# A spectral filter and an expert layer on one core: the first block's down matmuls by quarters, four input loads at other steps, one turn ahead of a piece

## The chip, the core and the metric

The kernel runs on one core of a Trainium2 chip. The metric is the device time of one execution in microseconds (us); the reference is the median of three executions of the kernel before, 767.72 us. The engines are TensorE (PE in the profile; PEld is its weight load), VectorE (DVE), ScalarE (ACT), GpSimd (POOL) and SyncE (SP). Here POOL computes next to nothing: it issues one queue of DMAs (the input loads, the swaps of the filter product), and SP issues the other (tables, transposing round trips through DRAM, output stores).

## The reference

Two layers, one behind the other. The first filters every channel of every batch in the frequency domain; the second is a feed-forward layer with a learned slope below zero.

```python
X = np.fft.rfft(x, axis=1)                    # x: 8 batches, 3008 rows, 256 channels
F = (filt_r + 1j * filt_i)[None, :, :]
y = np.fft.irfft(X * F, n=x.shape[1], axis=1)

h = y.reshape(24064, 256) @ w_in              # 256 -> 2048
g = np.maximum(h, 0.0) + alpha * np.minimum(h, 0.0)
return (g @ w_out).astype(np.float32)         # 2048 -> 256
```

## The kernel before

The transform of 3008 points is split into 94 times 32, and each part is done as matmuls with constant tables. For one batch the pieces are, in order: **a** (94-point part, eight pieces of two matmuls, evicted by ScalarE into `asb`, written to DRAM by `save_a` and read back transposed by `turn_a` into `at`), **b** (32-point part, six pieces; VectorE multiplies the result with the filter twice, into `ww` and `uu`, and POOL issues four DMAs that bring the halves of `ww` to the other partitions: for batch 1 they add straight into `uu`, the argument `direct` of `piece_b`), **c** (inverse 32-point part, six pieces), a second round trip through DRAM (`turn_c`), and **d** (inverse 94-point part, `pair_d`), which leaves the filtered rows transposed in `yT`.

Batch 0 has a class of its own, `First`, that turns its data on TensorE in place of DRAM: `piece_t` and `half_t` turn, `half_d` and `pair_d` are its last stage, `first_d` the beginning of that stage.

The feed-forward layer runs over 48 blocks of 512 or 384 rows of `yT` (`Block`). A block's `up` has 16 steps; each multiplies by one slice of 128 columns of `w_in`, and after every second one ScalarE copies two banks to `gtb` (line 586); after every fourth VectorE has made one group of four slices of g (lines 589 and 591). There are thus four groups, and group i holds the slices k = 4i to 4i+3 that the down matmuls need. The very first block is different: `up4` goes through its 512 rows in two halves, so that its four groups become ready one after another at the very end of its steps (lines 608, 613 and 614).

A block's down matmuls, 16 slices k for each of four lanes `si` of 128 rows, 64 in all, are cut into 16 **units** of four matmuls, which stand in the list `todo` and are done between the ups of the next block. Before, a pair of lanes is done at a time: lane 0 with k = 0 to 7, lane 1 with k = 0 to 7, lane 0 with k = 8 to 15, lane 1 with k = 8 to 15, then lanes 2 and 3 in the same way. A pair has one PSUM bank (`op`, from the pool `psO` with two), which ScalarE copies to `osb` when the pair is done, and SP then stores it.

Everything is in an order written out by hand: the program's global **step** runs on from block to block, 16 to a block, and `plan[step]` lists the pieces of the transforms that are put in front of that step's up. Engines take their instructions in that order and each waits for its own inputs. From step 16 to 149 one unit of the block before is done at every step. What a step puts into the plan stays in the order of the `put` calls: within one step batch 1's entries come ahead of batch 2's. `load_x` (line 123 for batches 1 to 3) issues two DMAs on the POOL queue, each of 192 KB (fp16), for half of the rows of a chunk; a batch has four chunks, chunk c being read by the pieces a number 2c and 2c+1. The pool `p_x` has four buffers, so a chunk's buffer comes free when the chunk of the same number of the batch before has been through its two pieces.

The steps that matter here, as `plan_fft` is called before:

| what | steps |
|---|---|
| batch 1, pieces a; save and turn | 16, 18, ... 30; 30 and 31 |
| batch 1, pieces b | 40, 46, 52, 58, 63, 68 |
| batch 1, pieces c | 52, 58, 64, 70, 76, 80 |
| batch 2, loads of chunks 0 to 3 | 32, 40, 50, 56 |
| batch 2, pieces a | 48, 54, 60, 66, 72, 74, 82, 84 |
| batch 3, loads of chunks 0 to 3 | 57, 69, 113, 123 |
| batch 3, pieces a | 106, 112, 118, 124, ... |

Of the kernel before, what the change touches and what calls it, by code (L numbers as in the profile page):

```python
# [11 lines left out]
FP32 = mybir.dt.float32  # L12
# [5 lines left out]
D = 256  # L18
# [3 lines left out]
AF = mybir.ActivationFunctionType  # L22
# [33 lines left out]
def kernel(  # L56
# [10 lines left out]
    nc = tc.nc  # L67
# [13 lines left out]
    psO = ctx.enter_context(tc.tile_pool(name="psO", bufs=2, space=bass.MemoryType.PSUM))  # L81
# [34 lines left out]
    def load_x(b, c, held=False):  # L116
        xs = p_x.tile([128, 8 * D], FP16, name="xs")
        if held:
            for r in (slice(0, 32), slice(64, 96)):
                nc.vector.memset(xs[r, 0:2], 0.0)  # L120
        if b:
            for r in (slice(0, 48), slice(48, N1)):
                nc.gpsimd.dma_start(out=xs[r], in_=xrow(b, c)[r])  # L123
        else:
            w = 8 * D // (1 + (c == 3))
            for o in range(0, 8 * D, w):
                nc.gpsimd.dma_start(out=xs[0:N1, o : o + w], in_=xrow(b, c)[:, o : o + w])
        return xs

    def load_halves(b, c):  # L130
        lo, hi = (p_x.tile([128, 8 * D], FP16, name="xs") for _ in range(2))
        nc.gpsimd.dma_start(out=lo[0:48], in_=xrow(b, c)[0:48])
        if b + 1 < NB:
            nc.gpsimd.dma_start(out=hi[0:48], in_=bass.AP(
                tensor=x.tensor, offset=x.offset + (b * NFFT + 47 * N2 + 8 * c) * D, ap=[[N2 * D, 48], [1, 8 * D]]))
        else:
            nc.gpsimd.dma_start(out=hi[0:32], in_=xrow(b, c)[47:79])
            nc.gpsimd.dma_start(out=hi[32:47], in_=xrow(b, c)[79:94])
        return lo, hi
# [26 lines left out]
    class Fft:  # L166
        def __init__(self, b):
            self.b = b
            self.base = (b % 2) * NFFT
            self.wi = wi3_s if b else wif_s  # L170
            self.uw = {}
# [290 lines left out]
    f0 = First()  # L462
# [89 lines left out]
    def store(p, t0, osb, lane):  # L552
        t = t0
        while t < t0 + 128:
            b, r = 2 * p + t // NFFT, t % NFFT
            g, o = r // NX, r % NX
            n = min(t0 + 128 - t, NX - o)
            row = b * NFFT + (o // 4) * N2 + 4 * g
            nc.sync.dma_start(
                out=bass.AP(tensor=out.tensor, offset=out.offset + row * D,  # L560
                            ap=[[N2 * D, n // 4], [D, 4], [1, D]]),
                in_=osb[t - t0 : t - t0 + n, lane])
            t += n
# [3 lines left out]
    class Block:  # L567
        def __init__(self, p, t0, tn):
            self.p, self.t0, self.tn = p, t0, tn
            self.gts, self.gs = [], []  # L570

        def up(self, j):
            tn = self.tn
# [40 lines left out]
                nc.vector.tensor_add(g, g, m)  # L614
                self.gts += [g[:, h] for h in range(4)]

        def start_down(self, last):
            n = self.tn // 128
            ends = [2, 3, 4] if last else list(range(2, n, 2)) + [n]
            half = 12 if last else 8  # L620
            self.todo = []
            for s0, s1 in zip([0] + ends, ends):
                for ks in (range(half), range(half, 16)):
                    self.todo += [(s0, s1, si, k) for si in range(s0, s1) for k in ks]

        def down(self, q):
            n = self.tn // 128
            for s0, s1, si, k in self.todo[n * q : n * (q + 1)]:
                if si == s0 and k == 0:
                    self.op = psO.tile([128, 2, D], FP32, name="op")  # L630
                nc.tensor.matmul(self.op[:, si - s0], self.gts[k][:, 128 * si : 128 * si + 128],  # L631
                                 wout_s[:, k], start=(si == s0 and k == 0), stop=(si == s1 - 1 and k == 15))
                if k == 15 and si == s1 - 1:
                    m = s1 - s0
                    osb = p_osb.tile([128, 2, D], FP32, name="osb")
                    nc.scalar.activation(osb[:, 0:m], self.op[:, 0:m], AF.Copy)  # L636
                    for lane in range(m):
                        store(self.p, self.t0 + 128 * (s0 + lane), osb, lane)

# [2 lines left out]
    def put(step, fn, *args):  # L642
        plan.setdefault(step, []).append((fn, args))

    def put_h(step, fn, *args):
        put(step, fn, *args)
        psum[step] = psum.get(step, 0) + 1

    def plan_fft(b, a_at, ta, x_at, b_at, add, c_at, d_at):
        f = Fft(b)  # L650
        split = b > 3
        for q in range(6):
            put_h(c_at[q], f.piece_c, q)
            if q % 2 == 1:
                put(c_at[q] + 1, f.turn_c, q // 2)
        for q in range(6):
            put(b_at[q], f.piece_b, q, not add)
            if add:
                put(b_at[q] + add, f.piece_s, q)
        for i in range(8):  # L660
            put_h(a_at[i], f.piece_q if split else f.piece_a, i)
        for c in range(4):
            put(a_at[2 * c + 1] + split, f.save_q if split else f.save_a, c)
            if b in (2, 3):
                put(x_at[c], lambda b=b, c=c: xc.update({(b, c): load_x(b, c, b == 3 and c > 1)}))
            if split:
                x0, x1, x2 = x_at[c]
                put(x0, lambda b=b, c=c: xc.update({(b, c): load_halves(b, c)}))
                put(x1, f.less, c)
                put(x2, f.plus, c)  # L670
        w = NK // len(ta)
        for q, t in enumerate(ta):
            put(t, f.turn_a, nc.sync, w * q, w * q + w)
        for i in range(8):
            put(d_at[i], f.pair_d, i, on_act)
# [5 lines left out]
        nc.vector.tensor_scalar(alm_s, al_s, 1.0, -1.0, OP.mult, OP.add)  # L681

    put(1, f0.half_d, 1, on_act, "o")
    put(1, f0.half_d, 3, on_dve, "o")
    put(1, f0.piece_t, 2, on_dve)
    for i in (6, 7):
        put(3, lambda i=i: on_dve(*f0.half_t(i, "o")))
    put(7, f0.pair_d, 2, on_dve)
# [12 lines left out]
    def d_steps(p):  # L701
        return [p + t for t in (92, 94, 104, 108, 116, 120, 140, 152)]

    plan_fft(1, range(16, 32, 2), [31] * 4, None, (40, 46, 52, 58, 63, 68), 0, (52, 58, 64, 70, 76, 80),
             (93, 95, 98, 101, 114, 121, 142, 154))
    plan_fft(2, (48, 54, 60, 66, 72, 74, 82, 84), [90] * 4, (32, 40, 50, 56),
             (106, 116, 126, 136, 148, 158), 7, (116, 126, 136, 148, 158, 172), d_steps(96))
    for b in range(3, NB):
        p = 96 * (b - 1)
        if b == 3:  # L710
            a_at = (106, 112, 118, 124, 130, 132, 140, 144)
            x_at = (57, 69, 113, 123)
            ta = (155, 166)
        else:
            a_at = [p - 96 + t for t in (-34, -22, 2, 2, 14, 26, 38, 50)]
            x_at = [[p - 96 + t for t in r] for r in
                    ((-66 if b == 4 else -68, -52, -40), (-32, -18, -10), (-20, -4, 8), (4, 20, 32))]
            ta = (p - 39, p - 28)
        plan_fft(b, a_at, ta, x_at, range(p + 2, p + 74, 12), 8, range(p + 14, p + 86, 12), d_steps(p))
# [8 lines left out]
    last = 0  # L728
    blk = Block(0, 0, 512)
    for step in range(16):  # L730
# [4 lines left out]
                     8: [lambda i=i: f0.half_d(i, on_dve, "o") for i in (6, 7)]}.get(step, []))  # L735
        for fn, args in plan.pop(step, ()):
            fn(*args)
    blk.start_down(False)
    units.extend((blk, q) for q in range(16))
    step = 16  # L740

    for p, t0, tn in blocks[1:]:
        blk = Block(p, t0, tn)
        for j in range(16):
            n = psum.get(step, 0)
# [9 lines left out]
            if n:  # L755
                last = step
# [39 lines left out]
```

## Time and profile before

| what | value |
|---|---|
| three executions | 767.60, 767.72, 771.18 us; median 767.72 us |
| the profiled execution | 768.86 us |
| its span, first to last instruction | 767.1 us |
| TensorE busy | 756.9 us |
| VectorE busy | 633.9 us |
| ScalarE busy | 583.3 us |
| costliest line: down matmuls, 3008 | 431.1 us, 273 ns each |
| next: up matmuls, 1504 | 418.1 us, 375 ns each |
| DMA: SP's queue and POOL's queue | 69.50 MB and 29.49 MB |

The span is 1.8 us shorter than the execution's time; what lies around it is the same small start and end. All times below that look like a place (at 80.01) are microseconds from the span's start. Matmuls overlap in the array, so the mean time of one is longer than the distance from one start to the next: a group of four matmuls with 512 columns has 0.86 us from its start to the start of what follows, one of four with 256 columns 0.43 us, when nothing holds them up. A wait of TensorE is therefore read from the distance of two starts, against the same group elsewhere.

### The profile page before, as it was taken

The numbers are of one execution on the slowest core, as the hardware profiler recorded it, in microseconds if no ns is written. First come the engines' busy times: TensorE is split into PE (matmuls) and PEld (weight loads), VectorE is DVE, ScalarE is ACT, GpSimd is POOL, SyncE is SP. The second block draws the span as 40 slices with busy tenths as digits, with TensorE's granted clock in tenths as the row PEclk, the third lists the DMA queues.
The fourth block names the chain that finished last, engine by engine and source line by source line (L and its number), as shares of the span: only waits on it lengthen the run. The fifth ranks groups of instructions, "written<-read, shape, count | busy, mean of one in ns | idle before, by whom it ended". The sixth has DMA issues, their size and how long they took to land.

```text
span 767.1 us, 16602 instructions
## 1 busy us (share of the span) xinstructions
PE 756.9 (99%) x6553; PEld 507.3 (66%) x6553; DVE 633.9 (83%) x1163; ACT 583.3 (76%) x672; POOL 147.0 (19%) x277
## 2 busy tenths in 40 slices
PE   8999999999999999999999999999999999999998
PEld 4666657666666666666666666766666666766666
DVE  4898975889889998899978998999877888666663
ACT  4788788888778777887778787787777777776664
POOL 6610840221211220121202122022101212000000
PEclk9999999999999999999999999999999999999999
DMA  9996996665752559533774438544463223510111
GB/s 162 157 225 173 175 204 181 166 171 139 178 153 69 139 142 197 143 97 97 188 205 96 125 104 179 166 97 118 131 162 87 71 68 97 152 36 28 42 42 56
DMA packets 97486, 100.04 MB, mean 130 GB/s; under 512 B 12086, under 2 KB 83398, under 8 KB 97216
## 3 DMA queue, kind: packets, MB, share of 16 engines
q1 hardware_dynamic: 82384, 69.50, 31.1%
q0 software_dynamic: 15024, 29.49, 21.4%
q8 instruction: 51, 0.84, 0.4%
q14 instruction: 27, 0.22, 0.1%
HBM read 55.02 MB, written 46.66 MB: 133 GB/s over the span
## 4 chain that ended last, share of the span: by engine, by line
PE 91%; DMA 4%; POOL 2%; DVE 1%; ACT 1%; issue 1%; SPq 0%; POOLq 0%; DVEq 0%; ACTq 0%
PE op L631 41%; PE hps L577 40%; PE psF L291 3%; PE hps L269 2%; PE psF L238 1%; PE hps L184 1%; DMA xs<-in_x_dram 1%; DMA uu<-ww 1%; PE hps L210 1%; DMA a_dram<-asb 1%; PE hps L600 1%; POOL filt_s L147 1%; DMA filt_s<-in_filt_r_dram 1%; POOL uu L250 1%; ACT asb L313 0%
## 5 line engine op out<-in xcount | busy, mean ns | idle before, releaser
L586 ACT ACTIVATE gtb<-hps 128x1024 f16<-128x1024 f32 (+1 forms) x376 | 377.9, 1007 | 132.6 <-PE hps L577 129.7
L631 PE MATMUL op<-wout_s,gtb 128*128 128x256 f16 x3008 | 431.1, 273 | 0.6 <-DVE gtb L614 0.6
L577 PE MATMUL hps<-yT,win_s 128*128 128x512 f16 (+1 forms) x1504 | 418.1, 375 | 0.3 <-ACT asb L313 0.2
L631 PEld LDWEIGHTS <-gtb 128*128 128x128 f16 x3008 | 290.8, 98 | 164.8 <-issue 10.7
L589 DVE TENSOR_SCALAR m<-gtb,alm_s 128x512 f16<-128x512 f16 (+1 forms) x752 | 227.3, 346 | 97.6 <-ACT gtb L586 96.1
L591 DVE TENSOR_TENSOR gtb<-gtb,m 128x2048 f16<-128x2048 f16 (+1 forms) x188 | 226.1, 1203 | 10.4
L577 PEld LDWEIGHTS <-win_s 128*128 128x128 f16 x1504 | 142.5, 98 | 54.9 <-issue 5.3
L252 POOL DMA_DIRECT2D sw<-ww x144 | 71.8, 506 | 414.2 <-DVE ww L245 399.4
L636 ACT ACTIVATE osb<-op 128x512 f32<-128x512 f32 (+1 forms) x97 | 56.6, 583 | 12.3 <-PE op L631 10.9
L313 ACT ACTIVATE asb<-hps 128x1024 f16<-128x1024 f32 (+1 forms) x56 | 56.7, 1020 | 6.4 <-PE hps L184 4.8
L245 DVE TENSOR_TENSOR ww<-psF,filts_s 128x1024 f16<-128x1024 f32 x42 | 51.2, 1219 | 1.0 <-DMA uu<-ww 0.7
L313 ACT ACTIVATE v<-hps 128x1024 f16<-128x1024 f32 (+1 forms) x43 | 43.5, 1012 | 11.2 <-PE hps L269 11.1
L246 DVE TENSOR_TENSOR uu<-psF,filt_s 128x1024 f16<-128x1024 f32 x42 | 51.1, 1216 | 0.0
L313 ACT ACTIVATE yT<-psF 128x752 f16<-128x752 f32 (+1 forms) x59 | 46.5, 788 | 1.7 <-PE psF L291 1.5
L291 PEld LDWEIGHTS <-zt 96*128 96x128 f16 x504 | 28.0, 98 | 5.8 <-issue 0.4
L291 PE MATMUL psF<-wi_s,zt 96*128 96x94 f16 x448 | 27.9, 205 | 0.0
L257 DVE TENSOR_TENSOR uu<-uu,sw 128x1024 f16<-128x1024 f16 x36 | 24.6, 683 | 1.3 <-DMA sw<-ww 1.3
L250 POOL DMA_DIRECT2D uu<-ww x24 | 19.6, 1174 | 28.1 <-DVE uu L246 21.4
L123 POOL DMA_DIRECT2D xs<-in_x_dram x24 | 17.6, 1009 | 12.9 <-DMA win_s<-in_moe_w_in_dram 4.5
L194 DVE TENSOR_TENSOR xs<-xs 47x2048 f16<-47x2048 f16 x16 | 19.5, 1219 | 0.4
L198 DVE TENSOR_TENSOR xs<-xs 47x2048 f16<-47x2048 f16 x16 | 19.4, 1210 | 0.0
L269 PE MATMUL hps<-uu,twi_s 64*64 64x256 f16 x336 | 17.6, 281 | 0.2 <-DMA uu<-ww 0.2
(99 smaller groups left out, 264.8 us busy)
## 6 DMA issues: line engine op xcount, KB each, us to landing
out_dram<-osb SPq DMA_DIRECT2D x128, 128.0 KB
v_dram<-v SPq DMA_DIRECT2D x84, 128.0 KB
zt<-v_dram SPq DMA_DIRECT2D x28, 384.0 KB
sw<-ww POOLq DMA_DIRECT2D x144, 64.0 KB, 2.7
xs<-in_x_dram POOLq DMA_DIRECT2D x40, 192.0 KB, 6.6
at<-a_dram SPq DMA_DIRECT2D x40, 192.0 KB
a_dram<-asb SPq DMA_DIRECT2D x32, 192.0 KB
a_dram<-asb SPq DMA_DIRECT2D x12, 384.0 KB
```

What stands on the lines that cost most here:

```text
L245: nc.vector.tensor_mul(ww, px, fs)
L246: nc.vector.tensor_mul(uu, px, f)
L252: nc.gpsimd.dma_start(out=sw[o : o + 32], in_=ww[i : i + 32])
L269: nc.tensor.matmul(ps[64 * par : 64 * par + 64, e, 256 * h : 256 * h + 256], twi_s[r, 4 * q + 2 * h + par], u[r, par, h], start=True, stop ...
L291: nc.tensor.matmul(ps[:, m], self.zt[:, 8 * g + 4 * mh + m, dh * 128 : dh * 128 + 128], self.wi, start=True, stop=True)
L313: nc.scalar.activation(o, i, AF.Copy)
L577: nc.tensor.matmul(self.hps[:, j % 2, 0:tn], win_s[:, kt, j * 128 : (j + 1) * 128], yT[:, kt, self.t0 : self.t0 + tn], start=(kt == 0), st ...
L586: nc.scalar.activation(g[:, 2 * i : 2 * i + 2], self.hps[:, :, 0:tn], AF.Copy)
L589: nc.vector.tensor_scalar(m[:, 2 * i + h], g[:, 2 * i + h], 0.0, a, OP.min, OP.mult)
L591: nc.vector.tensor_add(g, g, m)
L631: nc.tensor.matmul(self.op[:, si - s0], self.gts[k][:, 128 * si : 128 * si + 128], wout_s[:, k], start=(si == s0 and k == 0), stop=(si == ...
L636: nc.scalar.activation(osb[:, 0:m], self.op[:, 0:m], AF.Copy)
```

## The change

Three edits, and a small one that the first needs.

1. `start_down` of the first block takes a new argument: its 64 down matmuls are listed by quarters of k: all four lanes with k = 0 to 3, then all four with k = 4 to 7, and so on. Both pairs of lanes are now open at once, so `op` becomes a dictionary with one bank for each pair; both banks of `psO` are taken from unit 0 or 2 on, and the pairs end at units 13 and 15 in place of 7 and 15.
2. The loads of batch 2 move from steps 32, 40, 50, 56 to 40, 47, 56, 62, and the first two of batch 3 from 57 and 69 to 70 and 76.
3. In step 1 the turn `piece_t` number 2 comes ahead of `half_d` number 3. Both are evicted by VectorE.

```diff
@@ class Block
-            self.gts, self.gs = [], []
+            self.gts, self.gs, self.op = [], [], {}
...
-        def start_down(self, last):
+        def start_down(self, last, quarters=False):
             n = self.tn // 128
+            if quarters:
+                self.todo = [(s0, s0 + 2, si, k) for k0 in range(0, 16, 4) for s0 in range(0, n, 2)
+                             for si in (s0, s0 + 1) for k in range(k0, k0 + 4)]
+                return
...
                 if si == s0 and k == 0:
-                    self.op = psO.tile([128, 2, D], FP32, name="op")
-                nc.tensor.matmul(self.op[:, si - s0], self.gts[k][:, 128 * si : 128 * si + 128],
+                    self.op[s0] = psO.tile([128, 2, D], FP32, name="op")
+                nc.tensor.matmul(self.op[s0][:, si - s0], self.gts[k][:, 128 * si : 128 * si + 128],
...
-                    nc.scalar.activation(osb[:, 0:m], self.op[:, 0:m], AF.Copy)
+                    nc.scalar.activation(osb[:, 0:m], self.op[s0][:, 0:m], AF.Copy)
...
     put(1, f0.half_d, 1, on_act, "o")
+    put(1, f0.piece_t, 2, on_dve)
     put(1, f0.half_d, 3, on_dve, "o")
-    put(1, f0.piece_t, 2, on_dve)
...
-    plan_fft(2, (48, 54, 60, 66, 72, 74, 82, 84), [90] * 4, (32, 40, 50, 56),
+    plan_fft(2, (48, 54, 60, 66, 72, 74, 82, 84), [90] * 4, (40, 47, 56, 62),
...
-            x_at = (57, 69, 113, 123)
+            x_at = (70, 76, 113, 123)
...
-    blk.start_down(False)
+    blk.start_down(False, True)
```

## The prediction

> **What bounds the kernel.** I read the page first: busy times and the chain that ended last.
>
> ```profile
> PE 756.9 (99%) x6553; PEld 507.3 (66%) x6553; DVE 633.9 (83%) x1163; ACT 583.3 (76%) x672; POOL 147.0 (19%) x277
> PE 91%; DMA 4%; POOL 2%; DVE 1%; ACT 1%; issue 1%; SPq 0%; POOLq 0%; DVEq 0%; ACTq 0%
> ```
>
> TensorE is busy for 99% of the span and is 91% of the chain: time can only be won where TensorE waits, and every wait that is put into its order is paid in full unless another one goes for it. So I looked for waits in TensorE's timeline, around the steps that the edits touch.
>
> ```profile
> 43.94 1.02 PE L577 MATMUL hps<-yT,win_s 128*128 128x512 f16 x4
> 45.36 1.05 PE L631 MATMUL op<-wout_s,gtb 128*128 128x256 f16 x8 [0.40 <-DVE gtb L614]
> ...
> 71.30 0.30 PE L238 MATMUL psF<-at,twf_s 64*64 64x256 f16 x2
> 72.17 0.61 PE L577 MATMUL hps<-yT,win_s 128*128 128x512 f16 x2
> ...
> 80.01 0.60 PE L184 MATMUL hps<-xs,wf_s 94*96 94x512 f16 x2
> ```
>
> The columns are start, length, engine, line and form, and in brackets the idle time and who ended it. Four waits can be taken away, by the distance of starts against the same group unhindered: 43.94 to 45.36 is 1.42 where such a group takes 0.86, so 0.56 (edit 1: unit 1 needs group 1); 71.30 to 72.17 is 0.87 where batch 1's next piece b (77.48 to 77.83) takes 0.35, so 0.52 (edit 2); and, in rows of the same view not shown here, the piece c at 103.79 to 104.64 is 0.85 against 0.35 at 97.14, so 0.50 (edit 2), and the first four matmuls of `half_d` number 1 at 33.51 have number 3 only 0.65 behind them, at 34.16, where those four take 0.16 to what follows, so 0.49 (edit 3). Together 2.07 us. The row at 80.01 is batch 2's first piece a, step 48: TensorE gets there without a wait, because chunk 0 was asked for long before, as POOL's timeline shows.
>
> ```profile
> 57.42 1.39 POOL L123 DMA_DIRECT2D xs<-in_x_dram  x2
> 76.47 3.21 POOL L250 DMA_DIRECT2D uu<-ww  x4 [17.66 <-DVE uu L246]
> 78.55 2.19 POOL L123 DMA_DIRECT2D xs<-in_x_dram  x2
> 81.58 3.21 POOL L250 DMA_DIRECT2D uu<-ww  x4 [0.83 <-DVE uu L246]
> ```
>
> POOL runs ahead of TensorE where nothing holds it: the load of step 32 goes out at 57.42, when TensorE is at 62. But the load of step 40 goes out only at 78.55. Batch 1's first piece b is of step 40 too and stands ahead of it, so POOL first waits 17.66 us for `uu` and issues four swaps. That load is chunk 1 now, which TensorE needs at step 60 (92.69). After the change it is **chunk 0**, which TensorE needs at step 48.
>
> **Edit 2, the loads.** When does what is issued at that place land? The same line in that window:
>
> ```profile
> L123 POOL DMA_DIRECT2D xs<-in_x_dram x2: 1633/1642/1650, 78.6 to 79.1; - x2
> DMA to landing us min/median/max: 7.3/7.4/7.6
> ```
>
> The second half is issued at 79.1 and lands 7.6 later, at 86.7; the piece reads both halves. From the first swap's issue that is 86.7 - 76.47 = 10.2 us. The other two places where one chunk follows four swaps give 9.7 (81.58, last landing 84.2 + 7.1 = 91.3) and 10.4 (107.36, 110.0 + 7.7 = 117.7), though SP's traffic differs between the three. The swaps start when VectorE has made `uu`, and that moves with TensorE:
>
> ```profile
> 62.54 5.64 DMA a_dram<-asb
> ...
> 71.83 0.41 PE psF L238 x6
> ```
>
> This is the chain ahead of that piece b: batch 1's last save takes 5.64 us beside chunk 0's load, which lands at 57.9 + 9.5 = 67.4, and the read back from DRAM is what TensorE waits for at 71.83. Without that load the save should be quicker. But edit 1 puts the first pair's eviction (0.59 on ScalarE) and its two stores, which stand at 53.91 and 54.53 now, ahead of this very save: unit 13 ends at step 29, the save is of step 30, and the save's eviction and SP's queue both wait for them, some 0.6 us. VectorE's product cannot start before its own work of step 39 in any case. I take g = 0.5 us for how much earlier `uu` is ready, with bounds -0.3 (stores ahead, nothing saved) and 1.0 (0.56 + 0.52, what TensorE can be early by). So chunk 0 lands at 86.7 - 0.5 = **86.2**, with bounds 76.47 - 1.0 + 9.7 = 85.2 and 76.47 + 0.3 + 10.4 = 87.2. TensorE starts the piece then in place of 80.01: **+6.2** (5.2 to 7.2). What is queued behind the waiting matmul is everything: ups, units, the pieces of all later steps; ScalarE and VectorE run dry behind it.
>
> All that TensorE wins ahead of step 48, from any edit, only lengthens this wait. It arrives at some 79.3, so the wait is about 6.9 us long.
>
> Waits that long cost a second time. TensorE starts this kernel at half speed:
>
> ```profile
> 2.53 3.12 PE L468 MATMUL op<-ids 128*128 128x512 f16 x7 [2.53 <-DMA ids<-c_id]
> ...
> 7.04 1.89 PE L468 MATMUL op<-ids 128*128 128x512 f16 x8
> ```
>
> Seven of the same matmul run at 0.42 us from start to start, later ones at 0.216: 7 x 0.21 = 1.5 us lost until full speed. And the last view, of the busy time by windows with the granted clock behind the engines, shows that idleness brings this back: the last matmul ends at 759.80 + 3.77 = 763.6, and at the end the mean clock is 0.54 and not 1.
>
> ```profile
> 766.60:767.10 0.50, 0.00 (x0) 0.00 (x0) 0.00 (x0) 0.00 (x0) 0.00 (x0) 0.54 0.00 0
> ```
>
> The clock thus fell about 3.0 us after the last matmul. A wait of 6.9 us is over twice that, so I add **+1.5**, with bounds 0 and 3.0 (two such starts). The Trainium skill, page "TensorE: Matmul & The Clock Gate", section "Part 1: The HAM clock gate", says that the clock halves after at least one idle window of about 3.4 us and that these windows run free, not from the last matmul. By that rule a wait of 6.9 us nearly always holds a whole window and one of 5 us about every second time; by its figure the restart would cost some 1.7 us, an estimate, in place of 1.5.
>
> Behind step 48: chunk 1 (step 47) follows the second piece b's swaps and would land near 91, step 60 now comes at 92.69 + 6 or later: no wait. Chunks 2 and 3 have 16 and 20 steps. The load of batch 3 that stands ahead of the fourth piece b's swaps now goes, so its piece c (103.79) no longer waits: **-0.5** (bounds 0 and -0.5). Batch 3's two chunks now both follow the last piece b and share the queues with `turn_c`, which feeds the pair at 125.88; that row has no wait today, and I price it at 0, up to +0.7 if the transfers there are slowed (batch 3's chunk 1 alone lands at 117.7 today, two chunks some 3 us later, when the writes issued at 118.1 are under way).
>
> **Edits 1 and 3.** The number of matmuls, evictions and stores is the same. Unit 1 no longer needs group 1, -0.56; unit 0 still needs group 0, and its wait stays. VectorE can't follow:
>
> ```profile
> 44.00:62.00 18.00, 17.60 (x135) 11.62 (x134) 17.73 (x34) 14.75 (x16) 3.95 (x7) 1.00 0.96 221
> ```
>
> The third busy time is VectorE's, 17.73 of 18.00 us. The turn at 51.91 needs the bank that VectorE clears at 50.37 + 1.22 = 51.59, so 0.32 at most is kept past that. Edit 3 fills 0.49 with the turn's eight matmuls, but VectorE's eviction of `half_d` then comes 1.21 later, and the turn after it (35.64) waits for that bank: between -0.3 and +0.3, I take 0. Whatever is left is swallowed at step 48: both are worth **0**. That cover is the late load; if it is gone they are worth up to -1.05.
>
> **The sum**, for the profiled execution: 6.2 + 1.5 - 0.5 = +7.2, 768.9 to 776.1. That execution lies 1.1 above the median of 767.7, so the measured median should be **774.9**.
>
> **Rivals.**
> A. Late load, but the clock stays up, since the drop is only shown at the start and the very end: +5.7, 773.4. For it: no wait of TensorE over 1 us exists in the middle today, so nothing shows how soon the clock falls there.
> B. The load lands much sooner, because chunk 0 is no longer under way and SP's burst of reads ends earlier. Where no swaps crowd the queue a half lands in 3.7 us:
>
> ```profile
> L123 POOL DMA_DIRECT2D xs<-in_x_dram x2: 514/523/532, 146.7 to 147.2; - x2
> DMA to landing us min/median/max: 3.7/3.7/3.7
> ```
>
> Then 79.1 - 0.5 + 3.7 = 82.3, +2.3, the wait is 3.0 and the clock hardly falls, with -0.5 later: +1.8, 769.5. Against it: all three rows behind swaps have 6.7 or more. The page "DMA: Bandwidth & Descriptors" of the Trainium skill, section "Anatomy of one DMA", fits 2.0 us plus bytes by 436 GB/s for such a DMA; by that a half (393 KB read) would take 2.9, an estimate, and the sum would be +1.0. The rows behind swaps show more than twice that.
> C. Not slower: chunk 0 is there at step 48 and the four waits go: 767.7 - 2.07 = 765.6. It decides if the load lands by 79.3, that is 6.9 us earlier than my 86.2; it would need POOL to issue it ahead of the swaps, which the order of step 40 speaks against.
> D. A second late chunk or the slowed `turn_c` on top, with the longer restart: +7.2 + 0.7 + 1.5 = +9.4 or more, 777 to 779.
>
> **Chances.** Forecast 0.64, A 0.16, B 0.08, C 0.06, D 0.06. The forecast's own range is 5.2 - 0.5 = +4.7 to 7.2 + 3.0 = +10.2, 772.4 to 777.9. With a part of B at the low end the range that should hold 8 of 10 is 771.0 to 778.2. A measurement of this kernel tells 0.5%, 3.8 us, from no change. Slower by more is over 771.6: forecast, A and D, less a little for a landing at the early end, 0.84. Within 0.5%: B, C and that little, 0.14. Faster: 0.02, since all four waits together are 2.07 us, less than 3.8.
>
> **What would show it.** In the changed kernel's timeline TensorE's first L184 behind the one near 60 starts at 85 to 87 with an idle time of 6 to 8 us in front, ended by the DMA `xs<-in_x_dram`; POOL issues only swaps and then that load from 57 to 79; the granted clock around 83 to 90 is below 1 and ups after the wait start 0.43 apart; unit 1 (45.36) follows its up directly. I am wrong if that L184 comes by 81, or if the clock column stays at 1.00 there.

## The result and the profile after

The changed kernel takes 778.63 us (median of five executions, 776.12 to 781.18), the one before 767.87 beside it: a ratio of 1.013, 95% interval 1.0096 to 1.0165. On another chip, in a later comparison, it was 777.29 against 768.98, 1.0108 (1.0093 to 1.0122). Between 8 and 11 us are lost. The profiled execution took 777.07 us with a span of 775.3, so the span grew by 8.2 us.

The page, busy times and chain:

```profile
PE 759.0 (98%) x6553; PEld 508.1 (66%) x6553; DVE 634.0 (82%) x1163; ACT 583.1 (75%) x672; POOL 146.5 (19%) x277
PE 93%; DMA 3%; DVE 2%; POOL 1%; ACT 1%; issue 0%; POOLq 0%; ACTq 0%
```

TensorE is busy 2.1 us longer, with the same 6553 matmuls, and the span has grown by more than that: both have to be explained. Who TensorE waited for (engine, line, releaser; total, times, longest):

```profile
PE hps L184 <- DMA xs<-in_x_dram: 6.5, 1, 6.5
PE op L468 <- DMA ids<-c_id: 2.5, 1, 2.5
```

The second is the start of the kernel, as before. The first is new: one wait of 6.5 us, for an input load, at line 184, the matmul of the pieces a. TensorE's timeline around it, and below it the row of before with which the last one is compared:

```profile
78.32 1.04 PE L635 MATMUL op<-wout_s,gtb 128*128 128x256 f16 x8
85.82 1.06 PE L184 MATMUL hps<-xs,wf_s 94*96 94x512 f16 x2 [6.47 <-DMA xs<-in_x_dram]
86.67 1.91 PE L577 MATMUL hps<-yT,win_s 128*128 128x512 f16 x4
...
92.32 0.41 PE L269 MATMUL hps<-uu,twi_s 64*64 64x256 f16 x8
```

```profile
84.07 0.41 PE L269 MATMUL hps<-uu,twi_s 64*64 64x256 f16 x8
```

85.82 is batch 2's first piece a, step 48, at 80.01 before: 5.81 us late. What follows runs at half speed (the ups' four matmuls take from 86.67 to 88.38, 1.71 us and not 0.86), and the piece c at 92.32 stood at 84.07 before: 8.25 us late. So 2.44 us were lost behind the wait. The granted clock, third column from the end in the view of busy times by windows (ahead of it the five engines, behind it the DMA share and GB/s), says why:

```profile
79.36:84.07 4.71, 0.00 (x0) 0.00 (x0) 3.36 (x5) 0.67 (x2) 4.13 (x9) 1.00 0.93 142
84.07:85.82 1.75, 0.00 (x0) 0.03 (x1) 0.00 (x0) 0.00 (x0) 1.46 (x3) 0.50 1.04 247
85.82:90.90 5.08, 5.08 (x16) 2.46 (x17) 0.62 (x2) 2.04 (x2) 0.00 (x0) 0.50 0.60 101
90.90:95.00 4.10, 4.10 (x42) 2.67 (x40) 2.35 (x4) 3.07 (x3) 0.00 (x0) 1.00 0.00 0
```

The clock falls to 0.50 at 84.07, 4.7 us into the wait, and comes back at 90.90, 5.08 us after TensorE went on: half of these 5.08, 2.5 us, are lost. The load itself, on POOL:

```profile
54.44 0.49 POOL L534 DMA_DIRECT2D filt_s<-filt_s  x1 [2.60 <-DMA filts_s<-filt_s]
76.42 3.20 POOL L250 DMA_DIRECT2D uu<-ww  x4 [21.49 <-PE hps L577]
78.53 2.16 POOL L123 DMA_DIRECT2D xs<-in_x_dram  x2
```

Before, a load went out at 57.42. Now POOL issues nothing from 54.9 to 76.4, since four swaps that wait for batch 1's first piece b stand in front. (The bracket names a matmul; the product `uu` of that piece b, which the swaps add into, runs on VectorE from 74.66 to 75.87, and the swaps go out 0.55 behind it.) And when it lands, the load's line in that window:

```profile
L123 POOL DMA_DIRECT2D xs<-in_x_dram x2: 1617/1631/1645, 78.5 to 79.0; - x2
DMA to landing us min/median/max: 5.9/6.3/6.6
```

The second half goes out at 79.05 and lands at 85.7, just ahead of the piece.

### The profile page after: what moved, and what is told of

It reads as the page before. It is cut to its first block, busy times and chain, and to the rows that moved or that the text cites. A ratio compares the mean times of both kernels' runs of the same rounds, so it can differ in the third digit from the quotient of the medians.

```text
span 775.3 us, 16600 instructions
## 1 busy us (share of the span) xinstructions
PE 759.0 (98%) x6553; PEld 508.1 (66%) x6553; DVE 634.0 (82%) x1163; ACT 583.1 (75%) x672; POOL 146.5 (19%) x277
## 4 chain that ended last, share of the span: by engine, by line
PE 93%; DMA 3%; DVE 2%; POOL 1%; ACT 1%; issue 0%; POOLq 0%; ACTq 0%
PE op L635 42%; PE hps L577 41%; PE psF L291 3%; DMA xs<-in_x_dram 2%; PE hps L269 2%; PE psF L238 1%; PE hps L184 1%; PE hps L210 1%; DVE gtb L614 1%; DVE m L613 1%; DMA filt_s<-in_filt_r_dram 1%; POOL filt_s L147 1%; PE hps L600 0%; DMA zt<-v_dram 0%; DVE zt L316 0%
## 5 line engine op out<-in xcount | busy, mean ns | idle before, releaser
L591 DVE TENSOR_TENSOR gtb<-gtb,m 128x2048 f16<-128x2048 f16 (+1 forms) x188 | 226.2, 1203 | 10.4
L184 PE MATMUL hps<-xs,wf_s 94*96 94x512 f16 x48 | 14.8, 391 | 6.5 <-DMA xs<-in_x_dram 6.5
```

## The experiments

The times are medians; each ratio is to the kernel before on the same chip, with its interval. It is taken from all executions of both, so it can differ a little from the quotient of the two medians.

| run | what it is | us | before | ratio |
|---|---|---|---|---|
| e1 | changed, chunk 0 at step 39 | 768.77 | 768.57 | 1.0005 (0.9996 to 1.0014) |
| e2 | loads moved alone | 776.43 | 768.57 | 1.0101 (1.0084 to 1.0117) |
| e3 | changed, 28 extra matmuls in the wait | 776.02 | 768.57 | 1.0091 (1.0072 to 1.0110) |
| e4 | changed, chunk 0 at step 46 | 781.00 | 768.57 | 1.0155 (1.0135 to 1.0176) |
| e5 | changed, first two pieces a later | 770.73 | 768.55 | 1.0031 (1.0019 to 1.0042) |
| e6 | changed, batch 3's loads back | 777.74, one execution | 768.55 | |
| e7 | e1 without the turn in front | 769.07 | 768.55 | 1.0003 (0.9993 to 1.0012) |
| e8 | quarters and turn, no load moved | 769.13 | 768.55 | 1.0012 (0.9999 to 1.0024) |
| e9 | changed, again | 777.29 | 768.98 | 1.0108 (1.0093 to 1.0122) |
| e10 | loads moved alone, again | 777.48 | 768.98 | 1.0111 (1.0098 to 1.0124) |
| e11 | changed, 24 extra matmuls | 776.38 | 768.98 | 1.0097 (1.0079 to 1.0114) |
| e12 | loads alone, chunk 0 at step 39 | 769.29 | 768.98 | 1.0005 (0.9996 to 1.0013) |

### e1: one step earlier

```diff
-    plan_fft(2, (48, 54, 60, 66, 72, 74, 82, 84), [90] * 4, (40, 47, 56, 62),
+    plan_fft(2, (48, 54, 60, 66, 72, 74, 82, 84), [90] * 4, (39, 47, 56, 62),
```

> The changed kernel with one number other: chunk 0 of batch 2 is loaded at step 39 in place of 40, so that it stands ahead of the four swaps of batch 1's first piece b on POOL's queue and not behind them; all else as changed. My theory (the place behind the swaps makes the load late, and the late load is the whole loss): POOL issues it near 55, the wait of 6.5 us ahead of step 48 is gone, the granted clock stays at 1.00, and the time is that of the kernel before less the waits that the other edits remove, 766 to 767.5 us. Rival 1 (the load is late because it was moved later at all, a matter of distance in steps): nine steps are hardly more than eight, the wait stays at 5 us or more, 775 us or more. Rival 2 (the loss comes from the first block's new order or from the loads of batch 3): 773 us or more.

768.77 us, the same as the kernel before. One number, one step, is the whole loss. But the 766 to 767.5 us of the forecast were not reached: what the other edits were to win does not show. In its timelines POOL issues the load at 55.86 and not at 78.53, ahead of the swaps, and TensorE finds it there:

```profile
55.86 1.03 POOL L123 DMA_DIRECT2D xs<-in_x_dram  x2
76.50 3.20 POOL L250 DMA_DIRECT2D uu<-ww  x4 [19.60 <-DVE uu L246]
```

```profile
79.52 0.60 PE L184 MATMUL hps<-xs,wf_s 94*96 94x512 f16 x2
```

The step in the plan differs by one, some 0.9 us of TensorE's time; the issue differs by 22.7 us. A step says in which order POOL gets its instructions, not when it runs them. Both rivals are out.

### e4: behind the next swaps

```diff
-    plan_fft(2, (48, 54, 60, 66, 72, 74, 82, 84), [90] * 4, (40, 47, 56, 62),
+    plan_fft(2, (48, 54, 60, 66, 72, 74, 82, 84), [90] * 4, (46, 47, 56, 62),
```

> The changed kernel with chunk 0 of batch 2 at step 46 in place of 40: behind the swaps of batch 1's second piece b instead of the first. My theory: the load goes out when that piece's swaps do, at 83 to 84 instead of 78.5, and lands near 90 to 91.5, so step 48 starts 4.5 to 6 us later than in the changed kernel and the time is 781 to 786 us, the clock falling once as before. Rival (landing is a matter of traffic, not of the place in POOL's queue): within 2 us of the changed kernel.

781.0 us, the lower end of the forecast. The load goes out at 84.21, and the wait becomes 9.72:

```profile
89.78 1.06 PE L184 MATMUL hps<-xs,wf_s 94*96 94x512 f16 x2 [9.72 <-DMA xs<-in_x_dram]
```

TensorE starts 3.96 us later than in the changed kernel, not 4.5 to 6: loads issued at this place land 4.6 to 6.5 us after their issue, as that view gives for the four halves. The span is 3.6 longer (778.9). The clock stays at 0.50 for 10.25 us here, one window of this view:

```profile
85.04:95.29 10.25, 5.51 (x17) 2.67 (x18) 0.61 (x2) 2.04 (x2) 2.38 (x5) 0.50 0.57 90
```

but of these only 5.51 lie behind the wait, so a wait that is 3.2 us longer costs hardly more by the clock: half of 5.51 is 2.8 us, against 2.5.

### e2 and e10: the loads alone

```diff
-    blk.start_down(False, True)
+    blk.start_down(False)
```

(and the turn back behind the piece, the single bank back; only the two lines with the loads' steps differ from the kernel before)

> The kernel before with the loads moved alone: no quarters, no turn ahead of the piece. My theory: all that the other two edits win ahead of step 48 is swallowed by the wait there, so this is as slow as the changed kernel, 776 to 781 us, with step 48's piece starting at 85 to 87 and a wait shorter by what TensorE arrives later. Rival (the edits add up, so that without the quarters and the turn their gain of some 0.5 to 1 us is missing): 0.5 to 1 us slower than the changed kernel. Rival 2 (the quarters cost): faster than the changed kernel by 1 us or more and no long wait.

> The loads moved alone, once more, now beside the changed kernel. My theory (what the quarters and the turn win ahead of step 48 is swallowed there): no slower than the changed kernel, and up to 1.7 us faster where its shorter wait, 5.7 against 6.6 us, holds one window of the clock less. Rival (the edits add up): 0.5 to 1 us slower than the changed kernel.

e2 took 776.43 us; beside the changed kernel, on one chip, 777.48 (e10) against 777.29 (e9). The whole loss is in the loads. As for the rest, times alone do not separate the 0.2 us from a gain of 0.5, and the profiles do not either. In e2 unit 1 waits for its group again and TensorE comes to step 48 at 85.67 - 5.51 = 80.16, where the changed kernel is there at 85.82 - 6.47 = 79.35. But e10, the same program as e2, is there at 85.64 - 6.26 = 79.38; of the two only e2 waited 1.3 us near its start for a table (line 451). So 0.8 us is what two executions of one program differ by, and no measure of the other two edits. All three start the piece when the load lands:

```profile
85.67 1.06 PE L184 MATMUL hps<-xs,wf_s 94*96 94x512 f16 x2 [5.51 <-DMA xs<-in_x_dram]
```

The profiles show something else that the forecast did not have. In all five executions that wait here with the load at step 40 and no work added (after, e2, e6, e9, e10), TensorE is ready for step 48 2.92 to 2.94 us after the first swap goes out, wherever that is between 76.42 and 78.72. So an execution that is late as a whole ahead of batch 1's first piece b sends out its load late by as much. What the wait does swallow is what TensorE wins and the swaps do not: in the changed kernel TensorE is through the first piece b 0.82 us sooner than before (the next row starts at 71.35, before at 72.17), and the first swap goes out only 0.05 sooner (76.42, before 76.47).

The shorter wait of e2 has the shorter fall of the clock, too: 3.42 us.

```profile
85.47:88.89 3.42, 3.21 (x10) 1.46 (x11) 0.00 (x0) 1.43 (x2) 0.88 (x2) 0.50 1.04 175
```

But e10 is the same kernel with a wait of 6.26, not the 5.7 expected, and a fall twice as long, and is 1.5 us of span slower: where the fall lies is a matter of the single execution. Of the expected gain of up to 1.7 us over the changed kernel its median shows nothing.

### e3 and e11: work in the wait

```diff
+    put(48, lambda: warm(28, bank("h")))
     plan_fft(2, (48, 54, 60, 66, 72, 74, 82, 84), [90] * 4, (40, 47, 56, 62),
```

The extra matmuls (24 of them in e11) are added work whose result nobody reads.

> The changed kernel with 28 extra matmuls of 512 columns at step 48, ahead of batch 2's first piece a, into a PSUM bank that nobody reads: about 6.0 us of TensorE work in the place where it waits. They compute nothing that is used. My theory (the wait costs twice, by itself and by the clock that falls behind it): step 48's piece still starts at 85.5 to 86.5, but the granted clock stays at 1.00, the ups behind it run 0.215 us apart, and the time is 2 to 5 us below the changed kernel's, 773 to 775 us, and repeats within 1 us, since the scatter of the changed kernel comes from where the fall of the clock lies. Rival (the clock's record says little, TensorE would be held by the drained ScalarE and VectorE anyway): the time stays at 776 to 781 us. If the extra work were simply added: 783 us.

> The changed kernel with 24 extra matmuls in the wait in place of 28, 5.2 us, so that they end before the chunk lands in most executions (28 ended at 85.57, the chunk landed at 85.36 in that profile). My theory: the granted clock stays at 1.00 or at 0.999, the time is 2 to 4 us below the changed kernel's on the same chip, and what is left over the kernel before, 6 to 7.5 us, is the late landing alone. Rival (extra work in the wait is no help, the scatter of the landings decides): within 1 us of the changed kernel.

In e3's profile the clock stays up through the wait and behind it:

```profile
79.53:85.57 6.04, 6.04 (x30) 2.75 (x28) 3.53 (x5) 0.84 (x2) 5.46 (x9) 1.00 0.95 162
85.57:90.00 4.43, 4.43 (x43) 2.83 (x42) 0.74 (x3) 2.96 (x3) 0.31 (x1) 1.00 0.71 116
```

With six us of work added this execution has a span of 772.7 us, against 775.3, and behind the piece it runs as fast as the kernel before (the table below): the clock's part of the loss is real and is shown. ScalarE and VectorE run dry in this wait as in the other, so that alone costs nothing.

The expectations on the median and the scatter did not come true. The median, 776.02, is 1 us over the range and at the lower end of what the rival gave (776 to 781); e2, on the same chip, has 776.43 with an interval that overlaps, so the medians show no gain. They only show that the work is not simply added (783). e3's four executions go from 774.52 to 777.12 although the mean clock of every one is 0.999 or 1.000, so something other than this fall of the clock scatters by some 2.6 us. The landing is a part of it: in the eight profiles with this load at step 40 (after, e2, e3, e5, e6, e9, e10, e11) its second half lands 5.7 to 7.3 us after its issue. And the extra work can end after it (in the profile it ended at 85.57, the load had landed at 85.36). e11 is 0.9 us below the changed kernel on its chip, not 2 to 4 but what the rival gave, and its intervals overlap: by time alone that run is inconclusive. In its profile the chunk landed late, at 87.1, 1.9 us after the extra work, and behind that TensorE ran at full clock.

What the clock costs is read better from within the executions: from the start of step 48's piece to the end of the span, all kernels have the same work to do.

| execution | piece of step 48 starts | span | from there to the end |
|---|---|---|---|
| before | 80.01 | 767.1 | 687.1 |
| e1 (39) | 79.52 | 766.1 | 686.6 |
| e8 (no load moved) | 79.74 | 766.9 | 687.2 |
| e3 (28 extra) | 85.57 | 772.7 | 687.1 |
| e11 (24 extra) | 87.13 | 774.2 | 687.1 |
| e2 (loads alone) | 85.67 | 774.2 | 688.5 |
| e10 (loads alone) | 85.64 | 775.7 | 690.1 |
| after | 85.82 | 775.3 | 689.5 |
| e9 (after, again) | 88.70 | 777.9 | 689.2 |
| e4 (46) | 89.78 | 778.9 | 689.1 |

With the clock up the rest takes 686.6 to 687.2 us, whether the piece starts at 80 or at 87; with the clock fallen 688.5 to 690.1, which is 1.4 to 3.0 more than the kernel before. Not all of that is the clock: e10's rest holds a wait of 0.98 at a later pair (see e6). From the piece of step 48 to that of step 54 it is 6.37 us before and 6.33 in e3 and e11, but 7.76 in e9, 7.90 in e2, 8.16 in e6, 8.81 after, 8.84 in e10 and 9.02 in e4: the clock alone costs 1.4 to 2.7 us.

### e5: the use later in place of the load earlier

```diff
-    plan_fft(2, (48, 54, 60, 66, 72, 74, 82, 84), [90] * 4, (40, 47, 56, 62),
+    plan_fft(2, (55, 57, 60, 66, 72, 74, 82, 84), [90] * 4, (40, 47, 56, 62),
```

> The changed kernel with batch 2's first two pieces a at steps 55 and 57 in place of 48 and 54; the load of chunk 0 stays at step 40, behind the swaps. My theory (what counts is the time from the landing to the use: landing 85.7, use at 79.2): seven steps with their pieces are some 6.5 to 7 us, so the piece comes just when the chunk lands, the wait is below 1 us, the clock does not fall, and the time is 767 to 769.5 us. Rival (the load at this place hurts by its traffic too, by holding up the swaps behind it): 771 us or more although the piece does not wait.

770.73 us, a ratio of 1.0031 where the changed kernel has 1.011 to 1.013, and yet 1.2 over the forecast and only 0.3 short of the rival's 771. The wait is gone: the piece starts at 87.11, the load lands at 79.9 + 7.0 = 86.9. Some 2.2 us are left over the kernel before. The profile shows new short waits around the piece, 1.2 us together by their brackets, ended by ScalarE, which has the evictions of pieces from steps 55, 57, 58 and 60 in a row:

```profile
87.11 0.60 PE L184 MATMUL hps<-xs,wf_s 94*96 94x512 f16 x2
...
88.83 0.59 PE L577 MATMUL hps<-yT,win_s 128*128 128x512 f16 x2 [0.67 <-ACT asb L313]
...
91.83 0.41 PE L269 MATMUL hps<-uu,twi_s 64*64 64x256 f16 x8 [0.24 <-ACT asb L313]
...
92.74 1.02 PE L577 MATMUL hps<-yT,win_s 128*128 128x512 f16 x4 [0.28 <-ACT gtb L586]
```

The kernel before has a load of the same size at this place (78.55) and loses nothing by it, so the large loss is the lateness. Whether the traffic has a part in the 2.2 us is not shown.

### e6: batch 3's loads back

```diff
-            x_at = (70, 76, 113, 123)
+            x_at = (57, 69, 113, 123)
```

> The changed kernel with batch 3's first two loads back at steps 57 and 69; the rest as changed. One look. My theory: the long wait at step 48 and the fall of the clock stay, and the time stays within the scatter of the changed kernel, 775 to 780 us. The wait of 0.6 us at batch 1's first pair of the last stage (134.17 in the changed kernel, ended by the transposing read) goes, since one chunk less shares the queues with the writes ahead of it, and the wait of 0.5 us at the fourth piece c comes back. Rival (the 0.6 us come from the late step 48 itself): that wait stays.

777.74 us in this one execution, so nothing says that these loads are a part of the loss. My account of the two short waits fell: the one at the fourth piece c did not come back (112.23 to 112.57, 0.34), and the one at batch 1's first pair of the last stage did not go.

```profile
134.80 0.51 PE L291 MATMUL psF<-wi_s,zt 96*128 96x94 f16 x8 [0.89 <-DMA zt<-v_dram]
```

It is 0.45 in the changed kernel, 0.98 in e10, 0.21 in e8 where no load was moved, and absent in the kernel before and in e1, but also in e4 and e11 where step 48 is late. Such a wait comes and goes from one execution to the next; neither theory predicts it, and what decides is open.

### e7, e8 and e12: the parts without the late load

```diff
-    plan_fft(2, (48, 54, 60, 66, 72, 74, 82, 84), [90] * 4, (40, 47, 56, 62),
+    plan_fft(2, (48, 54, 60, 66, 72, 74, 82, 84), [90] * 4, (32, 40, 50, 56),
...
-            x_at = (70, 76, 113, 123)
+            x_at = (57, 69, 113, 123)
```

(e8; e7 is e1 with `piece_t` back behind `half_d`, e12 is the kernel before with the loads of e1)

> The changed kernel with all loads where they were: quarters and the turn alone. My theory: no long wait, the clock stays at 1.00, unit 1 no longer waits (0.56 us), but VectorE is full there and the turn at 51.9 waits for 0.3, and the waits at 71 and 104 stay: the time is that of the kernel before within 0.5 us. Rival (the first block's order costs, two banks being open at once): slower than the kernel before by 1 us or more.

> The kernel of chunk 0 at step 39 without the turn ahead of the piece: quarters, loads at 39, 47, 56, 62 and 70, 76. My theory (the turn in front saves 0.49 us at 34 and costs 0.63 us at 36, where the next turn waits for the bank that VectorE clears later): the wait of 0.63 goes, that of 0.49 comes back, the time is that of the kernel before less 0.3 to 1.5 us, 767 to 768.3 us on a chip where that one has 768.5; not to be told from the kernel with the turn. Rival (the turn in front helps): 0.5 us slower than that one.

> The kernel before with the loads moved as in the change but chunk 0 at step 39, no quarters, no turn. My theory: no wait at step 48 and the clock at 1.00; the waits of 0.52 at the first piece b and 0.50 at the fourth piece c are gone or smaller, so it is the kernel before less 0 to 1 us: the same within the interval. Rival (moving the other loads costs): slower by 1 us or more.

769.13, 769.07 and 769.29 us against 768.55, 768.55 and 768.98: all three the same as the kernel before within their intervals; the gain of 0.3 to 1.5 us expected of e7 did not come. The first block's order is neither a loss nor a gain that these runs can tell. The waits named in the prediction do go in the changed kernel, but not each by the edit that it was put down to, and others appear. In e8, where no load is moved, the first piece b does not wait either (71.55 to 71.89, 0.34), though I had expected it to. In the changed kernel the turn in front fills 33.39 to 33.88, but the second half of the next turn then waits for the bank that VectorE clears 1.2 us later:

```profile
33.39 0.61 PE L409 MATMUL psF<-ids,v 128*96 128x128 f16 x8
33.88 0.33 PE L291 MATMUL op<-wif_s,zt 96*128 96x94 f16 x4
...
34.91 0.39 PE L409 MATMUL op<-ids,v 128*96 128x128 f16 x4
35.77 0.38 PE L409 MATMUL op<-ids,v 128*96 128x128 f16 x4 [0.47 <-DVE yT L316]
```

34.91 to 35.77 is 0.86 where four such matmuls take 0.22: 0.64 lost for 0.49 won. In e12 the fourth piece c still waits (0.5 at 104) though batch 3's load no longer stands ahead of its swaps, and in e6 it does not wait although that load is back, so that wait does not hang on that load alone. No version tried beats the kernel before.

## Why the prediction was right, and where it was off

**The late load: right, by its mechanism and its place.** Chunk 0 at step 40 is behind four swaps on POOL's queue; e1 shows that this place is the whole loss, e4 that a later place costs more, e2 and e10 that the loads alone cost as much as all edits together. The piece of step 48 starts at 85.82 where 86.2 was forecast, and that it is so close is in part luck. Two terms were off and partly cancel: `uu` was to be ready 0.5 us sooner, and VectorE's product was only 0.3 sooner (74.66 against 74.95) and the first swap went out at 76.42 against 76.47; the load was to land as long after its issue as before (7.6), and took 6.6. SP's reads of `at` began 2.3 us sooner (66.07 against 68.37), as the save, issued at 62.77 behind the two stores, needed 3.3 us in place of 5.64 and had no load beside it. I had seen that this could happen and gave the landing none of it; that the earlier reads are what shortened the landing is my reading, no run shows it by itself. And the term scatters: from the first swap's issue to the piece it is 9.4 us here and 8.4 to 10.0 in e2, e6, e9 and e10, where 10.2 was taken with bounds of 9.7 and 10.4. In e9 the piece starts at 88.70, over the upper bound, since that execution was late before the swaps.

**The clock: right in kind, too small.** "+1.5, with bounds 0 and 3.0" is the mis-sized term. From piece to piece it measures 1.4 to 2.7, and 2.4 to 2.5 in the profiled execution (half of 5.08). The price was taken from the start of the kernel, where matmuls 0.42 us apart show TensorE at half speed for 2.9 us, until 5.5. (The clock column of the kernel before has 1.00 from 2.50 to 5.50 all the same: at the start it does not show this, and the distance of the matmuls decides.) Behind a wait it was 3.2 us in e2, but 5.08 after and 5.51 in e4. The Trainium skill, page "TensorE: Matmul & The Clock Gate", section "Part 1: The HAM clock gate", has windows of 3.413 us that run free; the records at half clock are 3.42 us long in e2, 6.83 in the changed kernel and 10.25 in e4, whole multiples of that figure, and the traces agree with it. By that rule, as I read it now, work that starts inside a window has to see that window out and fill another, so up to two windows at half speed were to be expected behind a wait; the forecast took about one. Rival A, the clock staying up, is out in every execution of the changed kernel: their mean clocks are 0.996, 0.996, 0.993, 0.993 and 0.991, and no execution of the kernel before is under 0.998.

**The later terms.** The fourth piece c indeed did not wait any more in the profiled execution (112.04 to 112.38, 0.34, forecast -0.5), though e12 and e6 show that this was not the load's doing alone. The pair behind the transposing read came 0.55 late by the distance of starts (its bracket has 0.45), priced at 0 with 0.7 as its bound; in e6, one execution, it is there without batch 3's moved loads. The two terms cancel.

**Edits 1 and 3 at 0: the number is right, the reason is not shown.** Unit 1 now follows its up without a wait (44.70), the turn at 51.53 waits 0.3 for VectorE as worked out, the turn in front gains 0.49 and costs 0.64. TensorE is ready for step 48 0.7 us sooner than before, but in e10, without these two edits, it is so too. "All that TensorE wins ahead of step 48, from any edit, only lengthens this wait" is too wide: it fits what TensorE wins at the first piece b, but what shifts the whole stretch ahead of that piece moves the load by as much (2.92 to 2.94 us from the first swap to step 48 in five executions). And the cover "if it is gone they are worth up to -1.05" was too hopeful: in e8 and e1, where no wait swallows them, they are worth nothing that can be told. So the 0 is in part luck: these edits would have been worth about 0 without the late load, too.

**The time.** 774.9 was forecast; the profiled execution's growth was 8.2 in place of 7.2, of which the clock is +0.9 to +1.0, the pair +0.55, the landing -0.4. The larger part of the miss is another: I took the median 1.1 us below the profiled execution, as it was before, and it was 1.6 above, 2.7 us of the 3.7 in all. So the median of five executions, 778.63, lies 0.4 over the upper end of the range; the second chip's 777.29 lies in it. That the profiled execution was among the fastest could not be known; that the executions would scatter could have been: both the landing and the free-running window differ from one to the next. Rivals B and C, a load that lands much sooner or in time, are out: of the profiled executions with the load at step 40 none has the second half landed before 85.3. Rival D came true in its smaller parts, the slowed pair and the longer restart, and its 777 to 779 us hold the median; but its second late chunk is not there, TensorE waits for one input load only.

## What to carry to other kernels

A step in a hand-written order is not a time: a DMA issue runs as early as its queue lets it, and behind an issue that waits for a product it is held until then. Before a prefetch is moved later, look for what else the same queue is given at that step, and compare the landing, not the issue, with the first use; here one step more or less was worth 8 to 11 us. And when the engine that bounds the kernel must wait, count the wait and the half-speed time behind it. Gains ahead of the wait need a second question: do they also bring forward what releases the prefetch? Here a shift of everything ahead of the product that the swaps wait for did, and what TensorE alone won did not.

## What the hardware showed beside that

With 6.0 us of matmuls added that nobody reads, the profiled execution is shorter: 772.7 us of span (e3) against 775.3. The medians do not show a gain. All of e3's executions have a mean clock of 0.999 or more; with 24 extra matmuls two of six have 0.998 and 0.997. The kernel before has 0.998 in two of its 17 executions on that chip, too, so it is not shown that the shorter cover let the clock fall.

The executions of the changed kernel are sorted by their mean granted clock: 776.12 and 777.07 us at 0.996, 778.63 and 779.92 at 0.993, 781.18 at 0.991. The order is no rule: when the changed kernel ran again (e9), 777.27 us had 0.993 and 777.21 and 777.31 had 0.996. One more fall can come from elsewhere: in e9's profile the clock is at half from 19.94 to 23.36, in the first block's transforms, behind 3.94 us in which TensorE was busy for 1.94.

```profile
16.00:19.94 3.94, 1.94 (x62) 1.21 (x64) 2.89 (x3) 1.82 (x3) 3.78 (x8) 1.00 0.95 128
19.94:23.36 3.42, 3.42 (x92) 2.22 (x86) 2.98 (x4) 2.42 (x4) 3.17 (x8) 0.50 1.02 141
```

What share of busy time keeps the clock up is not shown by this one case. A single execution may thus be 1.7 us slow, half of 3.42, with no change in the program; medians over several are needed to see what the short waits here are worth.
